# Attention and gated MLP on one core: a list scheduler in the source sets the order of all queues from the first MLP batch on

## The chip, the core and the metric

The kernel runs on one core of a Trainium2 chip. The metric is the device time in microseconds of one execution. The core has five engines with a queue of instructions each, which an engine works off in order: TensorE (PE in the profile; its weight loads are PEld), VectorE (DVE), ScalarE (ACT), GpSimd (POOL) and SyncE (SP), which here only issues DMAs. An engine waits at an instruction until the semaphores that it needs are there, and what stands behind it in the queue waits with it.

## The reference, cut to what matters

```python
scores = scale * np.matmul(q, k.transpose(0, 1, 3, 2))          # 8 batches, 8 heads, 576 tokens, 64 wide
cum = np.cumsum(np.log(np.clip(f, 0.0001, 1.0)), axis=-1)
decay = cum[:, :, :, None] - cum[:, :, None, :]
scores = np.where(causal, -1000000000.0, scores + decay)
attn = np.exp(scores - np.max(scores, axis=-1, keepdims=True))
attn = attn / (np.sum(attn, axis=-1, keepdims=True) + 1e-09)
x = np.matmul(attn, v)                                          # heads side by side: 576 x 512 a batch
h = np.maximum(x @ w_in, 0.0)                                   # 512 -> 1024
u, v = h[..., :512], h[..., 512:]
v_n = (v - mu) / np.sqrt(var + 1e-06)                           # mean and variance over the 512
v_s = np.einsum('ts,bsd->btd', w_spatial, v_n) + b_spatial[None, :, None]
return (u * v_s) @ w_out
```

## The kernel before, in words

Two heads form a pair; there are 32 pairs, four to a batch (`PPB`). The attention of pairs 0 to 3 and the scores of pair 4 run alone in `first` (about 74 us, ordered by hand). After that a loop at the end of the function draws from two generators, `attention(b)` and `moe(b)` (the gated MLP of one batch), so that the attention of batch b+1 is written in between the MLP of batch b. Within each queue the framework's scheduler then sets the order, from the order of the source and from its own estimate of durations.

A pair goes this way. SyncE loads `qk_t`, the decay rows `dk` and `dt`, and `vraw` (`prep`, `prep_v`). GpSimd masks `dk` and `dt` (`mask`, L280, L282, L286). TensorE makes the **first score piece** (three blocks of 128 queries with 384, 256 and 128 keys, L326, `sc<-qk_t`), then the **512 piece** (L326), then two **tail products** (queries 512 to 575 of both heads, `sc<-qk_t` with 288 columns, L233, since the helper `mm` records them). VectorE adds the decay and finds the row minimum (`lowest`, L306), ScalarE exponentiates and sums (L337; the tail L375), VectorE inverts the sums (L352, L353), and GpSimd multiplies the weights by them (`share`, L314). This multiplication I call a **share**; a pair has eight on `tt` and one on `tl`. They come after the 512 piece, since all four sums of a head are inverted together.

The weights must then be transposed. For pairs 0 to 7 TensorE does that (L414, L425) and ScalarE copies the result to `e` (L405). From pair 8 on (`moved`) VectorE transposes 32x32 blocks into `mid` (`move`, L456, L381) and SyncE puts the blocks in place with 16 DMAs from `mid` to `e` (`send`, L463); these need the product of the pair before to be done with `e`. The **product** with `vraw` (L480, from pair 8 on L488 and L493) writes two PSUM banks, which ScalarE (`xh`, L510) and VectorE (`xl`, L513) empty; `xh` and `xl` are the two fp32r parts of x.

The MLP of a batch multiplies in three terms (`xh winh`, `xh winl`, `xl winh`), all recorded as L233 with `ps`, `tp` or `sc` as target: first the v half token by token (`winh,xh` in the profile), followed by relu (L773), statistics (L774, L775), the root on GpSimd (L776, L777), normalization (`vx<-vx,mv`, L778) and the split into `vnh` (L780) and `vnl` (L782); then the u half (`xh,winh`); then the spatial product with `sph`, `spl`; then u times v_s (L823), its split into `gh` (L826) and `gl` (L827), and the product with `woh`, `wol`, copied to `o` and stored (L851, L853). In the first MLP batch the remaining weights are loaded and split too (`load_rest`, L126 to L144).

Of the kernel before, what the change touches and what calls it, by code (L numbers as in the profile page):

```python
# [15 lines left out]
PSUM = bass.MemoryType.PSUM  # L16
# [16 lines left out]

def f32(ap):
    return ap.bitcast(F32)


@with_exitstack
def attn_gmlp_kernel(ctx: ExitStack, tc: tile.TileContext, qk, v, f, w_in, w_sp, b_sp, w_out, out):
# [5 lines left out]
    nc = tc.nc  # L45
# [14 lines left out]
    ident = cst.tile([128, 128], F32, name="ident")  # L60
# [127 lines left out]
    own = {}  # L188
# [14 lines left out]
    def behind(i, j, sync=False):  # L203
        tc.add_manual_dep(i.ins, j.ins.name, mybir.DependencyInfo(
            mybir.DependencyClass.Sync if sync else mybir.DependencyClass.NoSync, mybir.DependencyReason.DATA),
            reason="order")

    freed, banks = {}, []

    def bank(n, piece=True):  # L210

# [5 lines left out]
    def in_one_piece(jobs, needs=()):  # L217

        was = None
        for job in jobs:  # L220
            if was is None:
                was = job()
                for j in [freed[n] for n in banks if n in freed] + list(needs):
                    behind(was, j, sync=True)
            else:
                with tc.high_priority():
                    i = job()
                behind(i, was)
                was = i
        banks.clear()  # L230

# [626 lines left out]
    def step(gen, done, t):  # L858
        try:
            return done + next(gen) / t, True  # L860
        except StopIteration:
            return round(done), False

    with tc.tile_pool(name="ws", bufs=2) as ws, tc.tile_pool(name="p0s", bufs=1, space=PSUM) as p0s, \
            tc.tile_pool(name="p0t", bufs=2, space=PSUM) as p0t:
        PS['s'], PS['t'] = p0s, p0t
        ws_.append(ws)
        first(ws)
        da, on = 1.0, False
    mo = ctx.enter_context(tc.tile_pool(name="mo", bufs=1, reuse_waits="tile"))  # L870
    for k, n in (("s", 1), ("t", 2)):
        PS[k] = ctx.enter_context(tc.tile_pool(name="ps_" + k, bufs=n, space=PSUM, reuse_waits="tile"))
    ps_m = ctx.enter_context(tc.tile_pool(name="ps_m", bufs=2, space=PSUM, reuse_waits="tile"))
    for b in range(B):
        gm = moe(b)
        dm, mon = 0.0, True
        while mon:
            while da < min(B, b + 1 + LEAD + dm):
                if not on:
                    gen, on = attention(int(round(da))), True  # L880
                da, on = step(gen, da, t_attn if b else t_first)
            dm, mon = step(gm, dm, t_moe)


# [41 lines left out]
```

## Time and profile before

| | |
|---|---|
| time, median of 3 runs | 758.35 us (758.02 to 760.0) |
| the profiled execution's own time | 758.39 us |
| its span, first to last instruction | 756.4 us |
| TensorE busy | 698.5 us (92% of the span), 4709 matmuls |
| VectorE, GpSimd, ScalarE busy | 481.2, 378.0, 369.6 us |
| mean granted TensorE clock | 0.984 |

The busy time of TensorE counts a matmul until its modelled end, so short waits between two of them don't show in it. The span is cut below into the part that `first` takes (to 74 us), the first MLP batch (to 160 us), the regular run of pairs and MLP batches (to 700 us) and the last MLP batch, in which no attention is left.

### The profile page before, as it was taken

What the parts mean: (1) busy time and instruction counts of PE and PEld (TensorE: products, weight loads), DVE (VectorE), ACT (ScalarE), POOL (GpSimd) and SP (SyncE); (2) the same over time, 40 slices, a digit from 0 to 9 for tenths busy, and PEclk for the clock granted to TensorE, in tenths of its full rate; (3) what the DMA queues carried; (4) which work ended last, traced back from release to release, by engine and by line L of the source; (5) the groups of instructions that cost most, each with busy time, mean ns of one, the idle gap of its engine ahead of it and who ended that gap; (6) DMA issues with size and microseconds to landing.
All of it is one profiled execution on the core that took longest, in us unless ns stands there. A gap on an engine that the chain in (4) does not pass through costs nothing.

```text
span 756.4 us, 14604 instructions
## 1 busy us (share of the span) xinstructions
PE 698.5 (92%) x4709; PEld 556.3 (74%) x4709; DVE 481.2 (64%) x1597; ACT 369.6 (49%) x1028; POOL 378.0 (50%) x703
## 2 busy tenths in 40 slices
PE   7878978799999998999998999999998898999997
PEld 3555757567788876877776877887787776788996
DVE  5888777954686648756776547756775556862421
ACT  5876686763544454533453344534563434641421
POOL 2887545582654426444644337354543446541411
PEclk9999999999999999999999999999999999999999
DMA  7855345245746865777576675776675675544001
GB/s 224 234 160 152 100 143 153 78 130 157 203 120 183 204 172 140 175 209 191 155 199 173 154 202 142 185 201 178 193 188 135 177 197 144 155 115 106 29 1 69
DMA packets 52749, 117.82 MB, mean 156 GB/s; under 512 B 10305, under 2 KB 14401, under 8 KB 52674
## 3 DMA queue, kind: packets, MB, share of 16 engines
q1 hardware_dynamic: 48082, 108.64, 53.8%
q10 hardware_dynamic: 4592, 8.26, 3.2%
q8 instruction: 37, 0.61, 0.4%
q14 instruction: 38, 0.31, 0.1%
HBM read 67.78 MB, written 9.75 MB: 102 GB/s over the span
## 4 chain that ended last, share of the span: by engine, by line
PE 41%; POOL 11%; DVE 9%; issue 8%; DMA 6%; ACT 5%; SPq 3%; POOLq 0%; ACTq 0%; DVEq 0%
PE ps L233 15%; PE tp L233 13%; POOL tt L314 5%; PE sc L326 5%; PE sc L233 4%; DMA dt<-rows_d 3%; PE sc L488 3%; ACT tt L337 3%; SPq L463 3%; DVE mid L456 2%; DMA dk<-rows_d 2%; DMA e<-mid 1%; DVE tt L306 1%; POOL vnl L782 1%; POOL gl L827 1%
## 5 line engine op out<-in xcount | busy, mean ns | idle before, releaser
L337 ACT ACTIVATE tt<-tt,nm 128x384 f32<-128x384 f32 (+2 forms) x240 | 132.7, 554 | 66.0 <-DVE nm L306 58.9
L314 POOL TENSOR_SCALAR tt<-tt,sm 128x128 f32<-128x128 f32 x208 | 108.0, 539 | 37.2 <-DVE sm L353 37.0
L456 DVE STREAM_TRANSPOSE mid<-tt 128x128 f32<-128x128 f32 x192 | 93.1, 500 | 40.3 <-POOL tt L314 34.6
L827 POOL TENSOR_TENSOR gl<-u,gh 128x256 fp32r<-128x256 f32 (+1 forms) x64 | 51.5, 805 | 107.3 <-ACT gh L826 106.7
L326 PE MATMUL sc<-qk_t 64*128 64x128 f32 (+3 forms) x512 | 90.1, 471 | 14.7 <-DVE xl L513 9.0
L306 DVE CUSTOM_DVE_ANT_1 tt<-sc,dk 128x256 f32<-128x256 f32 (+1 forms) x120 | 64.8, 550 | 23.1 <-PE sc L326 20.0
L326 PEld LDWEIGHTS sc<-qk_t 64*128 64x128 f32 x512 | 45.2, 190 | 39.1 <-DVE xl L513 11.3
L488 PE MATMUL sc<-e,vraw 128*64 128x256 f32 (+1 forms) x576 | 65.6, 348 | 4.6 <-DVE nm L306 1.7
L306 DVE CUSTOM_DVE_ANT_0 tt<-sc,dk 128x128 f32<-128x128 f32 (+1 forms) x120 | 48.8, 419 | 24.2 <-PE sc L326 22.6
L826 ACT CAST gh<-u 128x256 fp32r<-128x256 f32 (+1 forms) x64 | 27.0, 428 | 71.1 <-DVE u L823 34.6
L510 ACT CAST xh<-sc 128x256 fp32r<-128x256 f32 x64 | 25.1, 398 | 55.7 <-PE sc L488 31.9
L780 ACT CAST vnh<-vx 128x512 fp32r<-128x512 f32 (+1 forms) x40 | 24.7, 619 | 51.9 <-DVE vx L778 51.7
L782 POOL TENSOR_TENSOR vnl<-vx,vnh 128x512 fp32r<-128x512 f32 x32 | 41.3, 1298 | 15.0 <-ACT vnh L780 14.8
L776 POOL TENSOR_TENSOR mv<-mv,lnc 128x1 f32<-128x1 f32 (+1 forms) x40 | 8.4, 214 | 79.6 <-DVE mv L775 79.6
L280 POOL TENSOR_SCALAR_AFFINE_SELECT dk<-dk 128x256 f32<-128x256 f32 x60 | 25.4, 423 | 45.0 <-DMA dk<-rows_d 44.8
L233 PE MATMUL ps<-xh,winh 128*128 128x320 f32 (+1 forms) x136 | 42.9, 319 | 3.8 <-DVE vx L772 2.2
L774 DVE BATCH_NORM_STATS2 st<-vx 128x6 f32<-128x512 f32 (+1 forms) x40 | 27.1, 684 | 28.6 <-ACT vx L773 28.4
L337 ACT ACTIVATION_READ_ACCUMULATOR tt<-tt,nm 128x1 f32 x240 | 45.1, 188 | 0.0
L233 PE MATMUL sc<-qk_t 128*128 128x288 f32 x128 | 42.1, 425 | 1.9 <-DVE nm L306 1.9
L233 PE MATMUL ps<-sph,vnh 128*128 128x256 f32 (+1 forms) x144 | 43.8, 304 | 0.0
L233 PE MATMUL ps<-xh,winl 128*128 128x320 f32 (+1 forms) x136 | 41.3, 305 | 2.6 <-POOL winl L144 2.6
L488 PEld LDWEIGHTS sc<-e,vraw 128*64 128x64 f32 x576 | 32.4, 137 | 15.0 <-issue 4.9
(230 smaller groups left out, 2067.9 us busy)
## 6 DMA issues: line engine op xcount, KB each, us to landing
e<-mid SPq DMA_DIRECT2D x384, 100.0 KB, 2.2
qk_t<-in_dram SPq DMA_DIRECT2D x32, 608.0 KB, 6.6
dk<-rows_d SPq DMA_DIRECT2D x58, 320.0 KB, 4.4
vraw<-in_dram SPq DMA_DIRECT2D x32, 320.0 KB, 4.3
dt<-rows_d SPq DMA_DIRECT2D x58, 144.0 KB, 6.5
out_dram<-o ACTq DMA_DIRECT2D x28, 256.0 KB, 2.5
w<-in_dram SPq DMA_DIRECT2D x16, 256.0 KB, 3.0
w<-in_dram SPq DMA_DIRECT2D x4, 512.0 KB, 6.7
```

The source lines that it names most:

```text
L233: T.matmul(o, l, r, start=st, stop=sp)
L280: G.affine_select(out=two, in_=two, compare_op=ALU.is_ge, fill=-8.0 * BIG, base=0, pattern=[[0, 2], [-1, 128]], channel_multiplier=1)
L306: return V.tensor_tensor_reduce(out=out, in0=ps, in1=dec, scale=-0.125, scalar=3.0e38, op0=ALU.add, op1=ALU.min, accum_out=acc_)
L314: G.tensor_scalar(out=t, in0=t, scalar1=r, scalar2=1.0, op0=ALU.mult, op1=ALU.mult)
L326: return lambda: T.matmul(ps[:, c:c + n], qk_t[p, n - 128:n], qk_t[p, 640:640 + n], start=True, stop=True)
L337: last["exp", P, h, i] = A.activation(t, t, AF.Exp, bias=nm, scale=-1.0, accum_out=sm)
L456: V.transpose(out=part(middle(P)[:, 0, at:], [[32, n], [RUN, 4], [1, 32]]), in_=part(t, [[128, n], [32, 4], [1, 32]]))
L488: return lambda: T.matmul(out, vt[:, c, h, :], src, start=c == 0, stop=c == end)
L774: V.bn_stats(out=st[m, :], in_=x[m, :])
L782: G.tensor_tensor(out=tlo, in0=x, in1=f32(th[:]), op=ALU.subtract)
L826: A.copy(gh[j][:, 0:nt], g)
L827: G.tensor_tensor(out=gl[j][:, 0:nt], in0=g, in1=f32(gh[j][:, 0:nt]), op=ALU.subtract)
```

## The change

The new function `in_queues` runs at the end of the kernel function over all instructions written so far. It makes a step of every instruction (a score piece or a product is one step), finds what each step depends on from the memory it touches, gives it a duration by a table of linear costs (`cost`) and a delay until another engine sees its end (`SEEN`), and plans: at each turn it takes the engine that can start a ready step first, and of that engine's ready steps the one with the lowest rank. In the first plan the rank is the place in the source; then, three times, it is the latest start that still meets the end (`latest`), worked out backwards along the dependences and along TensorE's queue. A step that needs a new buffer waits until one of its kind is free (`PLACES`). Steps from before the first MLP batch count as done at time 0, with all engines free. The last plan's order is then laid down for each queue by dependences that order without a semaphore. No instruction's work is changed.

```diff
+PLACES = dict(GH=3, U=9, vnh=5, vnl=4, vx=2, st=2, mv=2, o=2, qk=2, xh=6, xl=6, nm=6, sm=6, tp=2, ps=2)
+SEEN = {"PE": 150, "DVE": 24, "Activation": 23, "Pool": 66, "SP": 17}
...
+def cost(i, e, ins, outs):
+
+    n = max([elements(b.ap) for b, _ in outs + (ins if i.opcode == "BNStats" else [])] or [1])
+    psum = any("PSUM" in str(b.tensor.space) for b, _ in ins)
+    op = str(getattr(i, "op", "")).split(".")[-1]
+    if i.opcode == "DMACopy":
+        name = outs[0][0].tensor.name.split("_")[0]
+        return {"e": 640, "out": 400}.get(name, 540), {"e": 2450, "qk": 5900, "raw": 5900, "dk": 4700, "dt": 5500,
+                                                     "vraw": 4000}.get(name, 3250)
...
+def in_queues(nc, tc, start, pieces, needs):
+
+    steps, of, own = [], {}, {i: p[0] for p in pieces for i in p[1:]}
+    W, R, users, tag_of, kinds = {}, {}, {}, {}, {}
+    for j, i in enumerate(nc.cur_bb.bb.instructions):
...
+    def lag(n, q):
+        return n.busy if n.e == q.e and not n.dma else n.done + SEEN[q.e]
+
+    def run(rank):
+
+        ready, free, mode = {e: [] for e in SEEN}, dict.fromkeys(SEEN, 0.0), None
+        when, at, left = [0.0] * len(steps), [0.0] * len(steps), [len(n.pred) for n in steps]
+        order, todo = {e: [] for e in SEEN}, {t: list(reversed(l)) for t, l in kinds.items()}
...
+        for _ in range(sum(not n.early for n in steps)):
+            best = None
+            for e, l in ready.items():
+                c = [(t, n) for n in l for t in (can(n),) if t is not None]
+                if c:
+                    t = max(free[e], min(t for t, _ in c))
+                    if best is None or t < best[0]:
+                        best = t, e, c
+            s, e, c = best
+            n = min((n for t, n in c if t <= s), key=lambda n: (rank[n.k], n.k))
+            ready[e].remove(n)
+            free[e] = s + n.busy
+            if e == "PE":
+                free[e] += 92 * (n.mode != mode)
+                mode = n.mode
+            at[n.k] = s
+            order[e].append(n)
+            take(n, s + n.done)
+            leave(n, s)
+        return at, order
+
+    def latest(at, order):
+
+        end = max(at[n.k] + n.done for n in steps if not n.early)
+        due, after = [end] * len(steps), {a.k: b for a, b in zip(order["PE"], order["PE"][1:])}
+        for n in sorted(steps, key=lambda n: -at[n.k]):
+            due[n.k] = min([end - n.done] + [due[q.k] - lag(n, q) for q in n.succ] +
+                           [due[q.k] - n.busy for q in (after.get(n.k),) if q])
+        return due
+
+    at, order = run([n.k for n in steps])
+    for _ in range(3):
+        at, order = run(latest(at, order))
+    for l in order.values():
+        l = [i for n in l for i in n.ins]
+        for a, b in zip(l, l[1:]):
+            tc.add_manual_dep(b, a.name, mybir.DependencyInfo(
+                mybir.DependencyClass.NoSync, mybir.DependencyReason.DATA), reason="order")
...
-    freed, banks = {}, []
+    freed, banks, pieces, needed = {}, [], [], []
...
+    early = len(nc.cur_bb.bb.instructions)
     mo = ctx.enter_context(tc.tile_pool(name="mo", bufs=1, reuse_waits="tile"))
...
                 da, on = step(gen, da, t_attn if b else t_first)
             dm, mon = step(gm, dm, t_moe)
+    in_queues(nc, tc, early, pieces, needed)
```

Where the change moves instructions is seen in the lists of the queues. On GpSimd, at the shares of pair 13, before (`tt_84` and `tt_85` are the weights of the two heads, `dk` the decay of pair 14):

```order
L280 AFFINE_SELECT dk<-dk 128x2x128
L314 TENSOR_SCALAR tt_84<-tt_84,sm 128x128
L782 TENSOR_TENSOR vnl<-vx,vnh 128x512
L314 TENSOR_SCALAR tt_84<-tt_84,sm 128x256
L314 TENSOR_SCALAR tt_84<-tt_84,sm 128x384
L314 TENSOR_SCALAR tt_84<-tt_84,sm 128x512
L314 TENSOR_SCALAR tt_85<-tt_85,sm 128x128
L314 TENSOR_SCALAR tt_85<-tt_85,sm 128x256
L314 TENSOR_SCALAR tt_85<-tt_85,sm 128x384
L314 TENSOR_SCALAR tt_85<-tt_85,sm 128x512
L282 AFFINE_SELECT dk<-dk 128x256
```

The same place in the changed kernel:

```order
L526 TENSOR_SCALAR tt_84<-tt_84,sm 128x384
L526 TENSOR_SCALAR tt_84<-tt_84,sm 128x256
L526 TENSOR_SCALAR tt_85<-tt_85,sm 128x384
L526 TENSOR_SCALAR tt_85<-tt_85,sm 128x256
L526 TENSOR_SCALAR tt_84<-tt_84,sm 128x128
L526 TENSOR_SCALAR tt_85<-tt_85,sm 128x128
L526 TENSOR_SCALAR tt_84<-tt_84,sm 128x512
L526 TENSOR_SCALAR tt_85<-tt_85,sm 128x512
L492 AFFINE_SELECT dk<-dk 128x2x128 x2
L494 AFFINE_SELECT dk<-dk 128x256 x2
L526 TENSOR_SCALAR tl<-tl,sm 128x576
```

The first mask of the next pair stood ahead of all shares and now stands behind the eight on `tt`. Over the 24 moved pairs a mask had four or more of the nine shares behind it in 20; now in 4, and in most of the others the last one or two.

On VectorE, at the moves of the same pair and the `xl` of pair 12, before:

```order
L456 STREAM_TRANSPOSE mid_2223<-tt_84 128x2x4x32
L456 STREAM_TRANSPOSE mid_2223<-tt_84 128x3x4x32
L456 STREAM_TRANSPOSE mid_2223<-tt_84 128x4x4x32
L456 STREAM_TRANSPOSE mid_2223<-tt_85 128x4x32
L456 STREAM_TRANSPOSE mid_2223<-tt_85 128x2x4x32
L456 STREAM_TRANSPOSE mid_2223<-tt_85 128x3x4x32
L513 TENSOR_TENSOR xl<-sc,xh 128x256
L456 STREAM_TRANSPOSE mid_2223<-tt_85 128x4x4x32
L513 TENSOR_TENSOR xl<-sc,xh 128x320
```

The same place in the changed kernel:

```order
L668 STREAM_TRANSPOSE mid_2223<-tt_85 128x4x32
L586 TENSOR_TENSOR nm<-nm 128x1
L986 BN_STATS st<-vx 128x6
L668 STREAM_TRANSPOSE mid_2223<-tt_84 128x4x4x32
L588 TENSOR_TENSOR sm<-sm,eps 128x1
L589 RECIPROCAL sm<-sm 128x1
L668 STREAM_TRANSPOSE mid_2223<-tt_85 128x4x4x32
L986 BN_STATS st<-vx 128x6
L725 TENSOR_TENSOR xl<-sc,xh 128x320
L725 TENSOR_TENSOR xl<-sc,xh 128x256
L668 STREAM_TRANSPOSE mid_2223<-tl 128x4x4x32
L593 STREAM_TRANSPOSE mid_2223<-tl 128x2x32
```

`xl` stands behind most moves in both; its two halves now come one behind the other, and the two moves of the tail close the pair.

On TensorE, from the first tail product of pair 14 to its 512 piece, before:

```order
L233 MATMUL sc<-qk_t 128x288
L233 MATMUL tp<-xh,winh 128x256
L233 MATMUL tp<-xh,winl 128x256
L233 MATMUL tp<-xl,winh 128x256
L233 MATMUL tp<-xh,winh 128x256
L233 MATMUL ps<-xh,winh 128x320
L233 MATMUL ps<-xh,winl 128x320
L233 MATMUL ps<-xl,winh 128x320
L233 MATMUL ps<-xh,winh 128x320
L326 MATMUL sc<-qk_t 128x512 x2
```

The same stretch in the changed kernel, from the 512 piece to the first tail product:

```order
L538 MATMUL sc<-qk_t 128x512 x2
L445 MATMUL ps<-xh,winl 128x320
L445 MATMUL ps<-xl,winh 128x320
L445 MATMUL ps<-xh,winh 128x320
L445 MATMUL ps<-xh,winl 128x320
L445 MATMUL ps<-xl,winh 128x320
L445 MATMUL sc<-qk_t 128x288
```

The 512 piece now comes first. In 9 of the 24 moved pairs the first tail product stood ahead of it; now in none.

## Rows read from the trace of the kernel before

**Rows 1.** The first line of the page.
```profile
span 756.4 us, 14604 instructions
```

**Rows 2.** Busy us of each engine (instructions) by stretch, clock, DMA share, GB/s.
```profile
74.00:160.00 86.00, 72.64 (x465) 55.05 (x462) 66.34 (x201) 58.27 (x167) 52.48 (x89) 0.96 0.42 124
160.00:700.00 540.00, 517.09 (x3583) 418.87 (x3582) 342.98 (x1172) 243.65 (x686) 259.02 (x494) 0.99 0.64 169
700.00:756.40 56.40, 51.38 (x312) 46.62 (x310) 15.91 (x37) 15.30 (x31) 15.30 (x22) 1.00 0.09 33
500.00:550.00 50.00, 50.00 (x349) 40.14 (x346) 31.35 (x112) 21.04 (x59) 26.44 (x54) 1.00 0.68 189
```

**Rows 3.** Waits of PE from 160 to 700 us: total us, times, longest.
```profile
PE sc L326 <- DVE xl L513: 8.0, 6, 2.7
PE tp L233 <- POOL gl L827: 2.8, 1, 2.8
PE ps L233 <- POOL gl L827: 2.2, 1, 2.2
PE ps L233 <- DVE vx L772: 2.0, 2, 1.0
```

**Rows 4.** Timeline of all engines, 281 to 297 us: start, duration, instruction, idle before.
```profile
283.66 0.41 POOL L280 TENSOR_SCALAR_AFFINE_SELECT dk<-dk 128x256 f32<-128x256 f32 x1 [3.24 <-DMA dk<-rows_d]
...
285.66 3.74 POOL L314 TENSOR_SCALAR tt<-tt,sm 128x256 f32<-128x256 f32 x7
...
286.61 2.73 DVE L456 STREAM_TRANSPOSE mid<-tt 128x256 f32<-128x256 f32 x6
...
290.19 0.45 DVE L513 TENSOR_TENSOR xl<-sc,xh 128x320 fp32r<-128x320 f32 x1
...
290.70 1.57 PE L326 MATMUL sc<-qk_t 64*128 64x384 f32 x12 [1.34 <-DVE xl L513]
```

**Rows 5.** Busy time by stretch around one long wait.
```profile
588.00:590.00 2.00, 0.00 (x0) 0.00 (x0) 1.86 (x6) 1.32 (x4) 2.00 (x5) 1.00 1.05 236
...
592.00:594.00 2.00, 2.00 (x9) 2.00 (x9) 1.25 (x4) 0.59 (x1) 0.92 (x2) 0.51 0.58 219
```

**Rows 6.** Two matmuls of PE, one behind the other.
```profile
285.40 0.39 PE L233 MATMUL tp<-winh,xl 128*128 128x512 f32 x1
285.63 0.40 PE L233 MATMUL ps<-winh,xh 128*128 128x512 f32 x1
```

**Rows 7.** Tail products of pair 14 on PE.
```profile
301.44 0.65 PE L233 MATMUL sc<-qk_t 128*128 128x288 f32 x2
```

**Rows 8.** SyncE’s queue from 300 to 345 us.
```profile
312.95 11.30 SPq L463 DMA_DIRECT2D e<-mid  x16
```

**Rows 9.** Pair 14’s product on PE, first and last row.
```profile
326.28 0.65 PE L488 MATMUL sc<-e,vraw 128*64 128x256 f32 x4 [1.32 <-DVE sm L376]
...
328.82 0.40 PE L493 MATMUL sc<-e,vraw 128*64 128x64 f32 x7
```

**Rows 10.** Second tail product of pair 31 on PE.
```profile
672.36 0.65 PE L233 MATMUL sc<-qk_t 128*128 128x288 f32 x2
```

**Rows 11.** SyncE’s queue from 670 to 690 us.
```profile
678.27 10.79 SPq L463 DMA_DIRECT2D e<-mid  x16
```

**Rows 12.** DMA issues on the page: count, KB, median us to landing.
```profile
e<-mid SPq DMA_DIRECT2D x384, 100.0 KB, 2.2
...
dk<-rows_d SPq DMA_DIRECT2D x58, 320.0 KB, 4.4
```

**Rows 13.** Timeline of all engines, 281 to 297 us, two normalizations.
```profile
292.57 0.51 DVE L778 TENSOR_SCALAR vx<-vx,mv 128x512 f32<-128x512 f32 x1
...
293.80 1.59 DVE L778 TENSOR_SCALAR vx<-vx,mv 128x512 f32<-128x512 f32 x1 [0.71 <-POOL mv L777]
293.81 1.30 POOL L782 TENSOR_TENSOR vnl<-vx,vnh 128x512 fp32r<-128x512 f32 x1
```

**Rows 14.** Timeline of POOL at the start of the first MLP batch.
```profile
74.55 1.36 POOL L314 TENSOR_SCALAR tt<-tt,sb 128x512 f32<-128x512 f32 x2
```

More of the change, by code (lines that the diff above doesn't have):

```diff
@@ L35, in f32, with __init__, elements @@
     return ap.bitcast(F32)
+PLACES = dict(GH=3, U=9, vnh=5, vnl=4, vx=2, st=2, mv=2, o=2, qk=2, xh=6, xl=6, nm=6, sm=6, tp=2, ps=2)
+SEEN = {"PE": 150, "DVE": 24, "Activation": 23, "Pool": 66, "SP": 17}
+class Step:
+    def __init__(self, k, e):
+        self.k, self.e, self.ins, self.pred, self.succ, self.tiles = k, e, [], set(), [], []
+        self.busy = self.done = 0.0
+        self.mode = self.dma = None
+def elements(ap):
+    n = 1
+    for _, k in ap[1:]:
+        n *= k
+    return n
@@ new lines, in touched @@
+def touched(b):
+    pitch = b.ap[0][0] or 1
+    at = [b.offset % pitch]
+    for s, k in b.ap[1:]:
+        at = [x + s * j for x in at for j in range(k)]
+    mask = 0
+    for x in at:
+        mask |= 1 << (x >> 2)
+    return b.offset // pitch, b.offset // pitch + b.ap[0][1], mask
+def cost(i, e, ins, outs):
[7 more added lines that the diff above has]
+    if e == "PE":
+        rows, cols = i.tile_size
+        slow = str(ins[0][1]) == "dt.float32"
+        if any(b.tensor.name.startswith("ident") for b, _ in ins):
+            t = 107
+        elif rows > 64 and cols > 64:
+            t = max(218, n * 1.667 + 8) if slow else max(111, n * 0.425 + 14)
+        else:
+            t = max(43, n * 0.888) if slow else max(55, n * 0.208 + 1)
+        return t, n * (0.92 if slow else 0.417) + 180
+    if e == "Activation":
+        t = (280 if len(outs) > 1 else 50 if psum else 185 if i.opcode == "Activation" else 100) + 0.83 * n
+        return t, t + 105
+    if e == "DVE":
+        t = 105 if n < 8 else (95 if i.opcode == "StreamTranspose" else 70) + (
+            0.8 if i.opcode == "TensorScalarPtr" else 1.06) * n
+        return t, t + 95
+    if i.opcode == "TensorTensor":
+        t = 520 if op == "pow" else 140 if n < 8 else 60 + 2.47 * n
+    else:
+        t = (240 if i.opcode == "TensorScalarPtr" else 140) + 0.84 * n
+    return t, t + 38
@@ L222, in in_one_piece @@
                 was = job()
+                pieces.append([was.ins.name])
                 for j in [freed[n] for n in banks if n in freed] + list(needs):
                     behind(was, j, sync=True)
+                    needed.append((was.ins.name, j.ins.name))
             else:
@@ L228, in in_one_piece @@
                 behind(i, was)
+                pieces[-1].append(i.ins.name)
                 was = i
```

86 lines of the change are left out of this document (added).

## The prediction

> **What bounds the kernel now.** I read the page first (span 756.4 us against 758.39 us for that execution, so 2.0 us lie outside the span) [rows 1], then the busy time by stretch [rows 2], then the waits of TensorE, and last the timeline at single waits. The reader should see in [rows 2] that TensorE is the engine that counts and that it is not always fed. From 160 to 700 us it is busy 517.09 of 540 us while VectorE is busy 342.98 and GpSimd 259.02, so these two have room on average. From 500 to 550 us it is busy 50.00 of 50 us at the full clock: the same work without waits exists in this very trace. From 74 to 160 us, where the remaining weights are split beside attention and MLP, it is busy only 72.64 of 86 us.
>
> What an order can give back is bounded by two things. Idle time: 86.00 - 72.64 = 13.4 us and 540.00 - 517.09 = 22.9 us. Clock: after an idle stretch (588 to 590 us, no matmul at all) TensorE was busy all of 592 to 594 us at a granted clock of 0.51, which is the lower level, 1.2 GHz [rows 5]. A wait of two microseconds is thus paid again in part. Over the two stretches the clock is 0.96 and 0.99 [rows 2], so at most 0.04 x 86 = 3.4 and 0.01 x 540 = 5.4 us. Together 45.1 us. The 5.0 idle us after 700 are the end of the program, where both orders do the same MLP, and the first 74 us are not touched by the planner.
>
> The waits are of a kind that an order makes. From 160 to 700 us TensorE's longest total is for `xl` before a first score piece, 8.0 us in 6 waits; then two single waits for `gl` of 2.8 and 2.2 us, the last subtraction ahead of the output product; 2.0 us for `vx`; 1.7 us for the row minimum that frees a tail product's bank [rows 3]. The idle time is 22.9 us, so some of it is spread over rows too small to list here, or shows only at weight loads.
>
> How one of them arises is in [rows 4]. At 283.66 us GpSimd starts the first mask of pair 14 after 3.24 us of waiting for the DMA of `dk`. The shares of pair 13 stand behind it, and seven of them run at 285.66 us. VectorE's six moves follow at 286.61 us; the second `xl` of pair 12 stands behind these moves and runs at 290.19 us; and the score piece, which needs the bank that `xl` reads, starts at 290.70 us after 1.34 us of idle TensorE. A DMA that TensorE does not need yet has held it up through two queues.
>
> **What the change does, part by part.**
>
> *Work.* No instruction is added or removed; the matmuls of the two queues add up to the same. 0 us.
>
> *GpSimd.* The masks no longer stand ahead of the shares in most pairs (20 of 24 before had four or more shares behind a mask, now 4 of 24). A wait like the 3.24 us [rows 4] then holds at most one or two shares and the tail. This is the main gain, since the shares feed the moves, the moves hold `xl`, and `xl` holds the score pieces.
>
> *TensorE's distances.* I add up TensorE's own work between two places in each order: 0.23 us for a 512-column matmul (start to start) and less in proportion [rows 6], 1.5 us for a first score piece [rows 4], about 0.5 us for a tail product (two records, overlapped by their ends) [rows 7], and 2.8 us for a pair's product (326.28 to 328.82 us and its last rows) [rows 9]. From the end of a product to the first score piece two pairs on, there were 3.9 to 7.0 us in 23 of the 24 moved pairs; now 4.7 to 6.8 in 19, with 1.6, 2.6, 3.4 and 3.4 as exceptions and one of 10.8. The chain there (copy, subtraction) is short if VectorE's queue is on time: 0.4 to 0.5 us for an `xl` [rows 4]. In 9 of 24 pairs the first tail product stood ahead of the 512 piece; now it follows by 0.7 to 2.2 us always, which gives the row minimum time. I expect the waits for `xl` and for the row minimum to go.
>
> *What gets tighter.* A pair's product needs all 16 sends of that pair, and these need the last move. In the old order 20.7 to 26.5 us of TensorE's work lie between the end of the second tail product and the product; in the new one 19.9 to 20.9 in 20 pairs and 16.9 to 18.1 in four. What the chain takes: the tail product of pair 14 ends at 301.44 + 0.65 = 302.1 us, the sends begin at 312.95, so 10.9 us later, take 11.30 us, and the product starts 2.0 us after them [rows 7 to 9]. That is 24.2 us, and this product was late: TensorE had been idle for 1.32 us. At pair 31, with no MLP statistics in the way, the sends begin 678.27 - 673.0 = 5.3 us after the tail product [rows 10, 11]. With 10.79 us of sends [rows 11] and the same 2.0 us this is 18.1 us, and a landing of 2.2 us at the median [rows 12] agrees with the last step. So the new order works if the sends begin within 20 - 13 = 7 us of the tail product. The trace has both ends, 5.3 and 10.9 us. Since the long one has the 3 us of mask waiting in its kind of queue and the new order removes that in most pairs, I take it nearer the short end, about 7 us, but with a spread: I charge 0.4 us of waiting in each of 24 pairs, 10 us. Bounds: nothing (5.3 us everywhere) and 24 x 3.9 = 94 us (10.9 us everywhere, which the masks' new place speaks against).
>
> *SyncE.* The sends are now 16 in one piece, ahead of the next `dk`, as before in most pairs. `dk` lands 4.4 us after issue [rows 12]. It is hidden while the masks come late; where one stands ahead of the last two shares, its lateness goes into the sends, and that is in the 0.4 us.
>
> *The seam.* The planner takes all engines as free at the first MLP matmul. The last shares of pair 4 end at 74.55 + 1.36 = 75.9 us [rows 14], while the new TensorE queue puts seven transposes of these weights behind the first three matmuls, 0.7 us after 74.1. I charge 1 us (bounds 0 and 2, the latter if the copies to `e` are late as well).
>
> *Weights split (74 to 160 us).* Here the waits have many causes (copies, splits, shares), and a planner that knows durations should fill a good part by pulling transposes and scores ahead, as it does from the first matmuls on. I take 60% of 13.4 + 3.4 = 16.8: 10 us. Bounds 3 and 15.
>
> *Sum.* 10 us up to 160; 22.9 + 5.4 - 10 = 18.3 us from there to 700; less 1 us at the seam: 27.3 us. 758.39 - 27.3 = 731.1 us, by the profiled time, which is the median (758.35) but for 0.04. **Predicted 731 us.** Its own range, from half to three quarters of the 45.1 us: 725 to 736.
>
> **A rule against it.** `vx` took 0.51 us at 292.57 and 1.59 us at 293.80, where it started with GpSimd's `vnl` (293.81, 1.30 us) [rows 13]; VectorE had to wait inside the instruction. The planner's table has one price for it. If each of the 32 whole normalizations ran beside `vnl`, VectorE would lose 32 x 1.08 = 35 us; it has 197 idle us from 160 to 700, so on TensorE's path only the last one or so of each batch counts, 8 x 1.08 = 9 us: 740 us. The Trainium skill (GPSIMD Engine Reference, section Key points) says that GpSimd shares its SBUF interfaces with VectorE and that they contend with VectorE instructions in a two-port mode or with two SBUF inputs. By that rule a tighter packing of the two engines lengthens both; the two rows agree with it for this one operation.
>
> **The rivals.**
> - *The waits move to the products* (sends late by 1 us rather than 0.4): 24 us are given back in place of 10, 745 us. For it: the sends of pair 14 already ended right ahead of their product [rows 8, 9], and three of the new distances lie below the 18.1 us. Against: a late product also delays everything behind it, which gives the next pair's sends more time.
> - *VectorE's normalizations stretch* (above): 740 us. For it [rows 13]; against, that they already do so before.
> - *Nearly all comes back*: 716 us, with 3 us of waits left. For it, the 50 us without a wait [rows 2]; against, that queues in a fixed order lose whenever one step is late and never win when it is early.
> - *No change* (758 us, within 0.3%): the order would have to lose as much as it wins, 1.1 us in each of 24 pairs on top of the 0.4.
> - *Slower*: the place is the product again. If the sends begin 9 us after the tail product, each product waits 2 us, and the clock falls behind such a wait [rows 5] for about 1 us more: 24 x 3 = 72 us lost against 37 us won elsewhere (10 + 28.3 - 1), 793 us at worst; with half of the pairs, 757. It decides from about 1.5 us of waiting a pair.
>
> **How the numbers follow.** Forecast 0.52, products 0.17, VectorE 0.09, nearly all 0.11, no change 0.04, slower 0.07. The first four are faster by over 0.3% (2.3 us, about what three runs can tell from no change): 0.89. The range leaves out the no-change and slower cases and the ends of the outer two: 714 (the floor is 713.3) to 748, a little beyond the products' case.
>
> **What would show it.** In the profile after: TensorE's busy time in 160 to 700 us closer to the length of the stretch, the wait for `xl` before score pieces gone or below 2 us, the waits of GpSimd for `dk` no longer followed by waits of VectorE for shares, first sends 6 to 8 us behind the tail product, and small waits at the products instead. The prediction is wrong if products wait over 1 us in most pairs, if the stretch to 160 us keeps its idle 13 us, or if waits shorter than the profile's idle rows show make the gain larger than 45 us.

## The result, and the profile after

The changed kernel takes 747.38 us (median of 4 runs, 746.35 to 747.91) where the kernel before takes 758.24 us beside it (median of 4, 758.02 to 760.0): a ratio of 0.985, with a 95% interval of 0.983 to 0.987. It is faster, by 11 us and not by the 27 us of the forecast, and the time lies at the upper end of the range. A second measurement, beside other runs of the kernel before, gave a ratio of 0.990 (0.986 to 0.993).

The first rows are the busy time by stretch of the profiled execution after the change (span 746.0 us), to be held against [rows 2]: length, then busy us of TensorE, weight loads, VectorE, ScalarE and GpSimd, each with its instructions, then TensorE's clock, DMA share and GB/s.

```profile
74.00:160.00 86.00, 71.28 (x447) 53.89 (x443) 70.92 (x193) 56.64 (x158) 52.19 (x81) 0.96 0.41 124
160.00:700.00 540.00, 525.70 (x3649) 425.62 (x3646) 341.02 (x1189) 252.98 (x699) 267.36 (x510) 0.99 0.65 171
```

From 160 to 700 us TensorE's idle time fell from 22.9 to 14.3 us. From 74 to 160 us it didn't fall at all: 14.7 us in place of 13.4. The starts of two pieces that have the same place in TensorE's work in both orders say the same: pair 11's first score piece starts at 227.1 us (before 225.8), pair 31's at 652.6 us (before 662.5). All of the gain lies between these two.

The waits of TensorE from 160 to 700 us, against [rows 3]: what waited for what, us in total, times, the longest.

```profile
PE tp L445 <- POOL gl L1039: 6.4, 3, 2.5
PE sc L538 <- DVE mv L987: 5.0, 5, 1.5
PE ps L445 <- POOL gl L1039: 1.8, 2, 1.4
PE sc L700 <- DVE mid L668: 0.6, 1, 0.6
```

The waits for `xl` are gone from the list, and the products (L700) wait 0.6 us in the whole stretch. But the waits for `gl` have grown from 5.0 to 8.2 us (6.4 and 1.8), and there is a new one: the 512 piece waits in each of five MLP batches, 5.0 us in sum, for a statistics step on VectorE. The largest wait for `gl`, on the timeline of GpSimd, SyncE and TensorE (start, duration, instruction, and in brackets the idle time before it with what ended it):

```profile
574.07 1.00 SPq L464 DMA_DIRECT2D dk<-rows_d  x2
...
578.71 0.41 POOL L492 TENSOR_SCALAR_AFFINE_SELECT dk<-dk 128x256 f32<-128x256 f32 x1 [0.79 <-DMA dk<-rows_d]
581.06 0.41 POOL L492 TENSOR_SCALAR_AFFINE_SELECT dk<-dk 128x256 f32<-128x256 f32 x1 [1.95 <-DMA dk<-rows_d]
581.42 0.77 POOL L494 TENSOR_SCALAR_AFFINE_SELECT dk<-dk 128x256 f32<-128x256 f32 x2
582.17 0.74 POOL L526 TENSOR_SCALAR tl<-tl,sm 128x576 f32<-128x576 f32 x1
582.89 0.69 POOL L526 TENSOR_SCALAR tt<-tt,sm 128x512 f32<-128x512 f32 x1
583.54 0.72 POOL L1039 TENSOR_TENSOR gl<-u,gh 128x256 fp32r<-128x256 f32 x1
...
584.32 0.50 PE L445 MATMUL tp<-woh,gl 128*128 128x512 f32 x1 [2.50 <-POOL gl L1039]
...
586.44 0.47 PE L445 MATMUL tp<-sph,vnh 128*128 128x320 f32 x1
586.71 0.47 PE L445 MATMUL tp<-spl,vnh 128*128 128x320 f32 x1
```

This is the pattern of [rows 4] once more, with other work behind it. GpSimd stands at a mask until the second `dk` lands, at about 581 us, 6.3 us after its issue in the trace (the plan's table says 4.7 for each `dk`; the first took 4.6). Behind the masks stand the tail share, the last share and `gl`, and TensorE waits 2.50 us for `gl`. Then it starts 320-column matmuls 0.27 us apart; in a kernel below, at the same place without the wait, 0.15 us apart. The granted clock behind the wait is 0.50, the lower level of 1.2 GHz:

```profile
585.00:588.00 3.00, 3.00 (x12) 2.80 (x11) 0.00 (x0) 1.03 (x2) 0.11 (x1) 0.50 0.75 192
```

The wait before the 512 piece is of the same make. At 374.65 us GpSimd starts a mask of `dt` after 2.30 us of waiting for its DMA. The two small steps on `mv` stand behind it, VectorE waits 2.85 us for them before its normalization, and the next statistics and the row minimum come after that; the 512 piece starts at 383.93 us after 1.51 us of idle TensorE.

```profile
374.65 0.23 POOL L498 TENSOR_SCALAR_AFFINE_SELECT dt<-dt 64x64 f32<-64x64 f32 x1 [2.30 <-DMA dt<-rows_d]
375.71 0.55 DVE L990 TENSOR_SCALAR vx<-vx,mv 128x512 f32<-128x512 f32 x1 [2.85 <-POOL mv L989]
```

### The profile page after: what moved, and what is told of

The parts are those of the page before. It is cut to its first block, busy times and chain, and to the rows that moved or that the text cites. A ratio compares the mean times of both kernels' runs of the same rounds, so it can differ in the third digit from the quotient of the medians.

```text
span 746.0 us, 14624 instructions
## 1 busy us (share of the span) xinstructions
PE 695.9 (93%) x4709; PEld 553.4 (74%) x4709; DVE 479.8 (64%) x1597; ACT 373.2 (50%) x1028; POOL 381.6 (51%) x703
## 4 chain that ended last, share of the span: by engine, by line
PE 62%; DVE 10%; POOL 7%; issue 4%; DMA 2%; ACT 1%; POOLq 0%; DVEq 0%; SPq 0%; ACTq 0%
PE ps L445 23%; PE tp L445 19%; PE sc L538 7%; PE sc L700 5%; PE sc L445 5%; POOL tt L526 3%; DVE tt L518 2%; PE sc L692 1%; PE sc L705 1%; DVE mid L668 1%; DMA dt<-rows_d 1%; DVE st L986 1%; POOL vnl L994 1%; POOL mv L989 1%; DVE vx L990 1%
## 5 line engine op out<-in xcount | busy, mean ns | idle before, releaser
L526 POOL TENSOR_SCALAR tt<-tt,sm 128x384 f32<-128x384 f32 (+3 forms) x208 | 110.4, 550 | 43.9 <-DVE sm L565 28.3
L538 PE MATMUL sc<-qk_t 64*128 64x128 f32 (+3 forms) x512 | 87.5, 460 | 9.9 <-DVE mv L987 5.0
L668 DVE STREAM_TRANSPOSE mid<-tt 128x384 f32<-128x384 f32 (+3 forms) x192 | 86.7, 486 | 9.7 <-POOL tt L526 8.7
L518 DVE CUSTOM_DVE_ANT_1 tt<-sc,dk 128x256 f32<-128x256 f32 (+1 forms) x120 | 62.2, 553 | 17.3 <-PE sc L538 17.0
L518 DVE CUSTOM_DVE_ANT_0 tt<-sc,dk 128x384 f32<-128x384 f32 (+1 forms) x120 | 46.8, 417 | 35.1 <-PE sc L538 33.5
L700 PE MATMUL sc<-e,vraw 128*64 128x256 f32 (+1 forms) x576 | 65.6, 348 | 0.7 <-DVE mid L668 0.6
L994 POOL TENSOR_TENSOR vnl<-vx,vnh 128x512 fp32r<-128x512 f32 x32 | 41.5, 1303 | 23.2 <-ACT vnh L992 22.9
L587 ACT ACTIVATE tl<-tl,nm 128x576 f32<-128x576 f32 x27 | 21.0, 777 | 51.4 <-DVE nm L586 51.4
L445 PE MATMUL ps<-spl,vnh 128*128 128x256 f32 (+1 forms) x144 | 42.5, 295 | 0.0
L445 PE MATMUL ps<-sph,vnl 128*128 128x256 f32 (+1 forms) x144 | 42.5, 295 | 0.0
```

What stands on the lines that cost most here:

```text
L445: T.matmul(o, l, r, start=st, stop=sp)
L518: return V.tensor_tensor_reduce(out=out, in0=ps, in1=dec, scale=-0.125, scalar=3.0e38, op0=ALU.add, op1=ALU.min, accum_out=acc_)
L526: G.tensor_scalar(out=t, in0=t, scalar1=r, scalar2=1.0, op0=ALU.mult, op1=ALU.mult)
L538: return lambda: T.matmul(ps[:, c:c + n], qk_t[p, n - 128:n], qk_t[p, 640:640 + n], start=True, stop=True)
L668: V.transpose(out=part(middle(P)[:, 0, at:], [[32, n], [RUN, 4], [1, 32]]), in_=part(t, [[128, n], [32, 4], [1, 32]]))
L700: return lambda: T.matmul(out, vt[:, c, h, :], src, start=c == 0, stop=c == end)
```

## The experiments

The idle times in the table are the length of the stretch less TensorE's busy time in each profile; the ratio is to the kernel before, run beside it on the same chip. The kernel before took 753.8 to 758.2 us in the five sets of runs, so the ratios are compared, not the times. The last column is the time from the first score piece of pair 4 to that of pair 11 in each profile. TensorE has the same matmuls between these two in all rows but the two with a star, where some more stand ahead of pair 11, about 3 us in the first and 8 us in the second (an estimate from 0.12 us between matmuls of 256 columns and 0.23 us between those of 512). Unlike idle time in a fixed window, this time also holds what a lower clock costs.

| Kernel | us | ratio (95%) | idle 74-160 | idle 160-700 | pair 4 to 11 |
|---|---|---|---|---|---|
| before | 758.24 | 1 | 13.4 | 22.9 | 164.8 |
| planned (the change) | 747.38 | 0.985 (0.983-0.987) | 14.7 | 14.3 | 166.2 |
| planned, second measurement | 747.18 | 0.990 (0.986-0.993) | 15.8 | 14.7 | 165.3 |
| prices of `dk` and `dt` raised | 731.48 | 0.971 (0.968-0.974) | 15.7 | 0.8 | 168.6 |
| price of `dk` alone | 730.42 | 0.969 (0.965-0.973) | 15.9 | 1.8 | 168.6 |
| price of `dt` alone | 740.41 | 0.982 (0.979-0.986) | 15.1 | 9.2 | 167.0 |
| raised, GpSimd's queue alone laid down | 730.66 | 0.969 (0.966-0.972) | 9.8 | 3.8 | 169.1* |
| raised, all queues but GpSimd's | 819.58 | 1.087 (1.084-1.091) | 16.9 | 57.6 | 179.8 |
| before, masks behind the last share from pair 9 | 731.99 | 0.973 (0.968-0.977) | 13.6 | 2.8 | 164.8 |
| the same from the first pairs on | 732.28 | 0.970 (0.966-0.974) | 12.7 | 2.7 | 165.8 |
| split priced double | 749.77 | 0.996 (0.993-0.999) | 17.9 | 14.7 | 170.3 |
| raised, split priced 1.3 times | 729.31 | 0.968 (0.964-0.971) | 16.2 | 0.7 | 168.0 |
| before, without VectorE's split | 742.89 | 0.986 (0.982-0.989) | 4.7 | 24.4 | 160.3* |
| planned, without VectorE's split | 740.08 | 0.982 (0.979-0.985) | 9.5 | 13.5 | 160.6 |
| raised, without VectorE's split | 717.70 | 0.952 (0.948-0.956) | 5.4 | 0.7 | 155.4 |
| raised, the maximum on GpSimd | 736.84 | 0.978 (0.974-0.981) | 17.3 | 2.2 | 171.8 |
| raised, without GpSimd's split | 726.54 | 0.963 (0.959-0.967) | 10.4 | 0.8 | 164.2 |

**Is the rest of the later stretch lost at the masks?** The table of landing times is all that is changed:

```
-"dk": 4700, "dt": 5500,
+"dk": 7500, "dt": 9000,
```

> The planned kernel with two prices raised in the table: the landing of `dk` 4700 to 7500, of `dt` 5500 to 9000. Theory 1 (what the later stretch lacks is lost where GpSimd's masks wait for a landing that the plan has too early, ahead of `gl` and of the two small steps on `mv`): TensorE's waits for `gl` at the output products and before the 512 piece, 14.9 us of idle in ten places by the timeline, shrink to below 4 us in all, the half clock behind them goes too, and the time falls by 8 to 14 us, to 733 to 740 us. Rival (a fixed order always meets some late step, whatever the prices): the waits turn up at other rows, the sum of idle time stays, and the time is 744 to 750 us. Up to 160 us both expect no change beyond 2 us.

Measured: 2.9% below the kernel before. Theory 1 holds. The stretch and the same place in the program as above:

```profile
160.00:700.00 540.00, 539.19 (x3793) 441.27 (x3790) 346.71 (x1201) 259.46 (x714) 271.48 (x515) 1.00 0.64 170
```

```profile
566.40 0.75 POOL L526 TENSOR_SCALAR tl<-tl,sm 128x576 f32<-128x576 f32 x1 [1.15 <-DVE sm L589]
567.45 0.74 POOL L1039 TENSOR_TENSOR gl<-u,gh 128x256 fp32r<-128x256 f32 x1 [0.30 <-ACT gh L1038]
568.14 0.41 POOL L492 TENSOR_SCALAR_AFFINE_SELECT dk<-dk 128x256 f32<-128x256 f32 x1
...
570.12 0.31 PE L445 MATMUL tp<-sph,vnh 128*128 128x320 f32 x1
570.27 0.31 PE L445 MATMUL tp<-spl,vnh 128*128 128x320 f32 x1
```

The tail share and `gl` now stand ahead of the masks, these find their `dk` landed, and TensorE is idle for 0.8 of 540 us at the full clock. No other wait took the place of those removed, as the rival had it.

Then each price alone.

> The planned kernel with the price of `dk` alone raised (4700 to 7500), that of `dt` left at 5500. Theory 1 (each wait has its own transfer: `gl` behind the masks of `dk`, the 512 piece behind the mask of `dt`): the waits for `gl` at the output products go (9.0 of 14.9 us), those of the 512 piece stay at 5 of 1.0 to 1.7 us, and the time is 1.9 to 2.5% below the kernel before. Rival (the place of the masks of `dk` decides over both): as with both prices raised, 2.7 to 3.1% below.

> The planned kernel with the price of `dt` alone raised (5500 to 9000), that of `dk` left at 4700. Theory 1, as mended by the run with `dk` alone (the masks of `dk` decide; those of `dt` follow them in the queue): the waits of the 512 piece for `mv` go, those for `gl` behind the masks of `dk` stay at 4 to 9 us, and the time is 1.6 to 2.4% below the kernel before. Rival (either price moves the masks far enough back): 2.7 to 3.1% below.

Measured: `dk` alone gives 3.1%, all of it, and of the waits of the 512 piece for `mv` one of 0.3 us is left; so "each wait has its own transfer" was wrong. `dt` alone gives 1.8% and leaves 5.7 us of waits for `gl`, as the mended theory expects, though 2.8 us for `mv` stay too, which it expected to go. The masks of `dt` follow those of `dk`, so the price of `dk` decides.

**Whose order brings the gain?** The same plan, laid down for a part of the queues (the first new line in one kernel, the second in the other):

```
-    for l in order.values():
+    for l in [order["Pool"]]:
+    for l in [order[e] for e in order if e != "Pool"]:
```

> The plan with the raised prices is made for all queues, but laid down for GpSimd's alone; the others take the order that they get without a plan. Theory of the prediction (the new place of the masks on GpSimd is the main gain, since shares feed moves, moves hold `xl`, and `xl` holds the score pieces): 11 us or more of the 22 us come, 1.5 to 2.5% below the kernel before, and the wait for `xl` before score pieces is below 3 us. Rival (the gain needs TensorE's new distances too): less than 5 us, 0 to 0.7% below the kernel before.

> The same plan laid down for all queues but GpSimd's. Theory of the prediction: with masks back ahead of shares over half of the 22 us is lost, 0.3 to 1.4% below the kernel before. Rival (TensorE's order carries the gain and draws GpSimd's queue after it): 2.2 to 3% below the kernel before.

Measured: GpSimd's queue alone gives 3.1%, all of the gain and more than the theory of the prediction expected (the framework's scheduler sets the other queues around it). All the other queues without it make the kernel 8.7% slower than before, worse than either expectation. In its trace GpSimd again has the first mask of `dk` ahead of four or more shares, in 11 pairs; but the kernel before has that in 20 and isn't as slow. The likely reason is that the others now stand in a fixed order that counts on GpSimd's planned one, so that each late share or `gl` holds up more; no run shows that by itself. GpSimd's waits from 160 to 700 us in that kernel:

```profile
POOL dk L492 <- DMA dk<-rows_d: 45.6, 22, 6.2
POOL dt L498 <- DMA dt<-rows_d: 34.9, 25, 3.0
```

and what TensorE then waits for:

```profile
PE tp L445 <- POOL gl L1039: 12.5, 4, 4.4
PE sc L538 <- DVE xl L725: 11.8, 6, 4.7
PE ps L445 <- POOL gl L1039: 8.9, 2, 4.7
```

**Are the masks enough?** No planner, one order by hand in the kernel before (`shared[P]` is the last share of a pair, its tail share):

```
 def mask(P, part=None):
     ...
+    if moved(P - 1):
+        for i in masks:
+            behind(i, shared[P - 1])
```

> The kernel before, without any planner, with one order added by hand: from pair 9 on every mask of a pair stands behind the last share of the pair before it on GpSimd. Theory 3 (the place of the masks is all of the gain from 160 us on; the list scheduler is only a way to find it): the waits for `xl` and for `gl` go, from 160 to 700 us TensorE is idle 4 us or less instead of 22.9, and the time is 2.2 to 3.2% below the kernel before. Rival (the other shifts on GpSimd that the plan makes, of `gl`, of the normalization and of the shares among themselves, are needed too): idle time of 8 to 16 us there, 0.8 to 1.9% below.

> The kernel before with the masks behind the last share of the pair before from the first pairs on, not only from pair 9 on; no planner. If the masks have no part in the stretch up to 160 us: within 0.4% of the same order from pair 9 on, 2.3 to 3.2% below the kernel before, TensorE idle there 12 to 15 us. If they have: idle 9 us or less there, 3.3 to 4% below.

Measured: 2.7% from pair 9 on, 3.0% from the first pairs on, idle time from 160 to 700 us 2.8 and 2.7 us, and no wait above 0.9 us in all from there (the first two rows of TensorE's waits, masks from pair 9 on):

```profile
PE sc L332 <- DVE xl L519: 0.9, 2, 0.7
PE sc L332 <- DVE nm L312: 0.7, 2, 0.3
```

Theory 3 holds: three lines (and the lists that name the instructions for them) do what the list scheduler does with the raised prices. The intervals overlap, so which is faster can't be told. The masks have no measurable part in the stretch up to 160 us: pair 11's first score piece comes 164.8 and 165.8 us after pair 4's, as before.

**Why did the stretch up to 160 us give nothing?** In the planned kernel VectorE is busy 70.92 of these 86 us. Its weight-split operations are longer beside GpSimd than alone. Eight rows of VectorE, GpSimd and TensorE in the planned kernel:

```profile
106.87 0.29 DVE L344 TENSOR_SCALAR wa<-wa 128x256 uint32<-128x256 uint32 x1
106.89 0.87 POOL L353 TENSOR_TENSOR winl<-w,winh 128x256 fp32r<-128x256 f32 x1 [0.84 <-ACT winh L352]
107.20 0.84 DVE L345 SCALAR_TENSOR_TENSOR w<-w,wa 128x256 uint32<-128x256 uint32 x1
107.72 1.45 POOL L994 TENSOR_TENSOR vnl<-vx,vnh 128x512 fp32r<-128x512 f32 x1
...
110.53 1.33 POOL L994 TENSOR_TENSOR vnl<-vx,vnh 128x512 fp32r<-128x512 f32 x1
110.76 1.26 DVE L344 TENSOR_SCALAR wa<-wa 128x256 uint32<-128x256 uint32 x1
112.11 0.42 DVE L345 SCALAR_TENSOR_TENSOR w<-w,wa 128x256 uint32<-128x256 uint32 x1
...
114.80 0.75 PE L445 MATMUL sc<-qk_t 128*128 128x288 f32 x2 [2.49 <-DVE nm L518]
```

L344 takes 0.29 us, and 1.26 us where it meets `vnl`; L345 takes 0.42 us, and 0.84 us where it meets GpSimd's L353, the last operation of another split. Behind them in VectorE's queue stand the row minima, and TensorE waits 2.49 us for one. First other prices for the five operations, 2.0 times with the first prices of the rows and 1.3 times with the raised ones. The table has 275 ns for each; with the raised prices they took 478 ns on average (38.2 us for 80), so that the two factors lie on both sides of the measured 1.74:

```
+        if n == 256 and i.opcode == "TensorScalarPtr":
+            t *= 2.0
```

> The planned kernel with one price changed: VectorE's operations of the weight split (256 elements, a scalar operand) cost double. Theory 2 (up to 160 us VectorE itself is too full, its split operations being stretched beside GpSimd, so an order can't win there): pair 11's first score piece starts at 227 us as in the planned kernel, within 2 us, and the time is 745 to 750 us. Rival (the order of that stretch is bad because the plan doesn't know the length of those operations): with the right price it is filled better, the piece starts 5 to 10 us earlier, and the time falls to 737 to 742 us.

> The plan with the raised prices, and VectorE's operations of the weight split priced at 1.3 times. Theory 2 (VectorE is full there, so a better price doesn't help): within 0.4% of the raised prices alone, 2.5 to 3.3% below the kernel before. Rival (a right price, unlike the double one, lets the plan fill the stretch): 3.5% or more below.

Measured: the double price gains nothing. It is 0.4% below the kernel before where the planned one is 1.0 to 1.5% below it, though its interval touches that of the second measurement, and pair 11 comes 170.3 us after pair 4, 4 to 5 us later than with the plan (in the profile its piece starts at 234.8 us). Theory 2 expected no change, the rival a gain. With 1.3 times nothing changes, as theory 2 has it. A price nearer the measured one doesn't help. Then the operations left out, in three orders:

```
-        V.tensor_scalar(out=af, in0=af, scalar1=2.0 ** -15, scalar2=None, op0=ALU.max)
-        V.tensor_scalar(out=a, in0=a, scalar1=3, scalar2=0x3FFFFFF8, op0=ALU.logical_shift_left, op1=ALU.bitwise_and)
-        V.scalar_tensor_tensor(out=w, in0=hi, scalar=0xC0000000, in1=a, op0=ALU.bitwise_and, op1=ALU.bitwise_or)
-        V.tensor_scalar(out=a, in0=w, scalar1=0xFF800000, scalar2=None, op0=ALU.bitwise_and)
-        V.scalar_tensor_tensor(out=af, in0=lo, scalar=2.0 ** -52, in1=af, op0=ALU.mult, op1=ALU.mult)
+        A.activation(wf, hi.bitcast(F32), AF.Abs)
```

> The kernel before, with VectorE's five operations of each of the 16 weight splits after the first 74 us left out (one more absolute value on ScalarE stands in for them), so that these weights are not the reference's. It takes 80 operations off VectorE, 40 us by their durations in the planned kernel. Theory 2 (VectorE is what fills the stretch up to 160 us): the stretch gets shorter by 5 to 10 us even in the old order, and the time is 748 to 754 us. Rival (the waits up to 160 us come from copies, landings and the order): 755 to 759 us.

> The planned kernel with the same operations left out, so that these weights are not the reference's. Theory 2: the plan now gets there what was forecast for it, TensorE's idle time from 74 us to pair 11 falls by some 10 us, and the time is 733 to 739 us, 12 to 18 us below the old order with the same operations left out. Rival (something else than VectorE holds the stretch up): 742 to 748 us, and the distance between the two orders stays at 11 us.

> The planned kernel with the raised prices of `dk` and `dt` and, as in the two kernels before it, without VectorE's five operations of each of the 16 later weight splits, so that these weights are not the reference's. With the raised prices TensorE is busy 499.19 of 500 us from 160 us on, so nothing later can hide or eat what the first stretch gives. Theory 2 (VectorE's stretched split operations make the stretch up to 160 us late): idle time there falls from 15.7 us to 9 us or less, and the time is 6 to 9 us below that of the raised prices, 3.6 to 4.1% below the kernel before. Rival (the planned order itself leaves TensorE without work there, whatever VectorE does): within 3 us of the raised prices, 2.6 to 3.3% below the kernel before.

Measured: in the old order 1.4%, a little more than theory 2 expected, and an idle time of 4.7 us up to 160 us; with the raised prices 4.8%, so 1.9% or 14 us more than the plan with these operations, twice what theory 2 expected. In the planned kernel with its first prices the idle time fell by 5.2 us only, and the two orders came within 0.4% of each other, which neither theory expected: the plan there loses 5.0 us up to 160 us at ScalarE's copies to `e`. Why it does so with these prices and not with the raised ones wasn't tried. The stretch with the raised prices, with and without the five operations:

```profile
74.00:160.00 86.00, 70.32 (x432) 54.19 (x432) 67.94 (x189) 55.47 (x156) 52.50 (x85) 0.92 0.39 123
```

```profile
74.00:160.00 86.00, 80.61 (x517) 63.28 (x517) 36.66 (x121) 65.22 (x189) 55.03 (x95) 0.96 0.43 134
```

So it is the split's operations on VectorE. Leaving them out also makes each split five steps shorter, though, and these three kernels alone can't tell VectorE's time from that. The waits of TensorE in the plan with the raised prices speak for VectorE's time (74 to 162 us, the five largest):

```profile
PE ps L445 <- ACT u L1013: 4.4, 2, 4.2
PE sc L538 <- DVE nm L518: 2.8, 1, 2.8
PE sc L538 <- DVE xl L725: 2.3, 1, 2.3
PE sc L692 <- DVE nm L518: 2.1, 2, 1.9
PE ps L445 <- DVE vx L984: 2.0, 1, 2.0
```
```profile
128.43 0.24 ACT L735 CAST xh<-xl 128x64 fp32r<-128x64 f32 x1 [2.21 <-DVE xl L725]
```

Four of the five end at VectorE, and before the long one for `u` ScalarE had itself stood 2.21 us waiting for VectorE's `xl`; none ends at a split weight. (In the old order one of 2.6 us does, for `winl`.) Is it the amount of VectorE's work, or the stretching? Two edits of the later splits: one of the five operations moved to GpSimd, and, in another kernel, GpSimd's two operations left out:

```
-        V.tensor_scalar(out=af, in0=af, scalar1=2.0 ** -15, scalar2=None, op0=ALU.max)
+        G.tensor_scalar(out=af, in0=af, scalar1=2.0 ** -15, scalar2=1.0, op0=ALU.max, op1=ALU.mult)
```
```
-        G.tensor_tensor(out=wf, in0=wf, in1=af, op=ALU.add)
-        G.tensor_tensor(out=dl, in0=wf, in1=f32(dh), op=ALU.subtract)
+        A.copy(dl, af)
```

> The plan with the raised prices, and one of VectorE's five operations of each later weight split, the maximum, done by GpSimd. Theory 2 (VectorE's load makes the stretch up to 160 us late; leaving all five out gave 14 us): a fifth of it, 2 to 4 us, 3.1 to 3.5% below the kernel before, with VectorE busy 5 to 8 us less from 74 to 160 us. Rival (what stretches VectorE's operations is GpSimd's work beside them, and more of that takes as much as it gives): no gain, 2.5 to 3.0% below.

> The plan with the raised prices, with GpSimd's two operations of each of the 16 later weight splits left out (ScalarE's copies stand in for one of them), so that these weights are not the reference's. It takes 32 operations of 0.73 us off GpSimd and none off VectorE. Theory 2a (VectorE is stretched by GpSimd's work beside it): VectorE's 80 split operations, 38.2 us in sum with the raised prices, take 31 us or less, idle time of TensorE up to 160 us falls from 15.7 us by 5 us or more, and the time is 3.6 to 4.4% below the kernel before. Theory 2b (it is the amount of VectorE's work): their sum stays above 34 us, or it falls and the idle time stays within 3 us; 2.5 to 3.3% below.

> The planned kernel as it is, on the chip of the runs beside it. All theories expect what it measured before, 1.3 to 1.7% below the kernel before, and so 8 to 11 us above the same plan with the raised prices.

Measured: with the maximum on GpSimd the kernel is 2.2% below the one before, less than either side expected and 0.6% worse than without that edit, though VectorE is busy 9 us less in the stretch. Moving work from VectorE to GpSimd doesn't make it faster. Without GpSimd's part it is 3.7% below, 0.8% better, and idle time falls by 5.3 us. VectorE's groups in this stretch (count, busy us, mean ns), first with the raised prices alone, then without GpSimd's part:

```profile
L345 DVE SCALAR_TENSOR_TENSOR w<-w,wa 128x256 uint32<-128x256 uint32 x16 | 9.4, 586 | 0.9
L344 DVE TENSOR_SCALAR wa<-wa 128x256 uint32<-128x256 uint32 x16 | 7.3, 453 | 0.5
L342 DVE TENSOR_SCALAR wa<-wa 128x256 f32<-128x256 f32 x16 | 6.6, 412 | 2.2 <-ACT wa L340 2.1
```

```profile
L345 DVE SCALAR_TENSOR_TENSOR w<-w,wa 128x256 uint32<-128x256 uint32 x16 | 8.0, 503 | 1.0 <-ACT winh L353 0.4
L344 DVE TENSOR_SCALAR wa<-wa 128x256 uint32<-128x256 uint32 x16 | 5.9, 368 | 0.5
L342 DVE TENSOR_SCALAR wa<-wa 128x256 f32<-128x256 f32 x16 | 4.8, 303 | 3.5 <-ACT wa L340 3.5
```

All 80 operations took 38.2 us and now take 32.5, between the two bounds. By time and idle time theory 2a fits. But the run also takes two steps out of each split's chain and gives GpSimd 22 us back (busy 52.50 before, 30.61 now), so how much of the 0.8% is the shorter operations and how much the shorter chain stays open. The planned kernel as it is came out at 1.0% below the one before, less than the 1.3 to 1.7% expected, and so 1.9% or 14 us above the raised prices, where 8 to 11 us were expected.

## Why the prediction was right and wrong

*The mechanism was right.* The masks on GpSimd hold shares, moves, `xl` and score pieces; "the main gain" was put there. GpSimd's queue alone, or three lines in the kernel before, bring all of the gain that any order brought. The waits for `xl` went as forecast. VectorE's waits for shares, from 160 to 700 us, fell from 56.5 to 17.7 us, but the chain from a late `dk` through a share to VectorE was not gone: behind the masks at 581 us VectorE still waited 2.55 us for the tail share. In the new trace four or more shares stand behind the first mask of the next pair's `dk` in one pair, where four were counted in advance.

*The step that failed* is "I take 60% of 13.4 + 3.4 = 16.8: 10 us" for the stretch up to 160 us. It measured nothing: idle time 14.7 for 13.4 us, clock 0.96 as before, pair 11 1.3 us later. That the stretch keeps its idle 13 us was one of the prediction's own signs of being wrong. The idle rows there were read as an order's fault. But VectorE was busy 66.34 of 86 us there [rows 2] and its split operations stretch beside GpSimd. Taking these away freed 8.7 us even in the old order (13.4 to 4.7), and 10.3 us in the plan with raised prices. No order or price tried there gave that: GpSimd's queue alone shows 9.8 us of idle time, but at a clock of 0.88, and pair 11 comes no earlier than in the kernel before (169.1 us after pair 4, with about 3 us more work ahead of it). The rival "VectorE's normalizations stretch" names a lengthening that the rows up to 160 us show as well, for other operations; from 160 us on VectorE had room enough for it (idle 0.8 us in the plan with raised prices, with the same operations), and up to 160 us, where it hadn't, the prediction didn't look for it. How much of the loss is the lengthening and how much the amount of VectorE's work stays open. The Trainium skill (SBUF — State Buffer, section Who interferes with whom) says that VectorE and GpSimd share a port pair that one of them holds for a whole instruction while the other is blocked, and that `tensor_scalar` can need it. The rows agree: L344 at 110.76 us ended 0.16 us after the `vnl` that had started 0.23 us before it.

*The term of 18.3 us* from 160 to 700 us was right in kind and came out at about 11 us (from pair 11 to pair 31: 9.9 + 1.3). What was charged against it, 10 us of small waits at the products, was wrong in place and in size: the products waited 0.6 us. In their stead about 13 us were waited for `gl` and before the 512 piece, and the half clock came behind some of these waits. The prediction saw that a mask could still stand ahead of the last two shares, as it does in 15 pairs of the trace, and put "its lateness into the sends"; it didn't follow GpSimd's queue on to `gl` and to the steps on `mv`, which stand behind the masks as well. With the masks' price mended, all 22.9 us of the idle rows but 0.8 came back, and the time from pair 11's first score piece to pair 31's fell from 436.7 to 407.0 us, by 29.7. So the 28.3 us from idle time and clock were a sound measure of what an order can give back in this stretch, and "nearly all comes back" was the right case for it, once the plan knew how long a landing takes.

*The sends.* The first sends began 4.8 to 9.5 us behind the tail product in the planned kernel, 17 of 24 within the 6 to 8 us that were named, and the products waited 0.6 us in all: the 7 us taken from the bounds 5.3 and 10.9 held, and the 0.4 us a pair charged on top did not come. The rival that the products take over the waits, and the slower case that rests on it, fall.

*The seam.* It was charged as 1 us, and from 74 to 80 us TensorE is idle for 0.6 us, waiting for a copy to `e`, where it had no idle time before. The rise from 74 to 100 us, from 1.5 to 5.0 us, is for the larger part two waits for row minima behind it, 1.56 and 2.43 us, which belong to the step that failed: VectorE is busy 9.26 us from 90 to 100 us.

## What to carry to other kernels

Where an in-order engine does work that waits for a DMA, look at what stands behind it in that queue, all of it and not only the first victim; a dependency of three lines that puts such work last did as much here as a scheduler for all queues with its best prices. A plan is as good as its longest waits are priced: a landing priced near the median of all put everything behind a mask at the mercy of the second of two transfers, and a landing priced too long cost little here (2 to 3 us from pair 4 to pair 11, against 18 us gained behind it). Before idle time is booked as an order's to give back, check that the engine it waits for has room in that very stretch, with the durations that its operations have there.

## What the runs showed of the hardware

Two transfers of `dk`, issued one behind the other in 1.00 us, landed 4.6 and 6.3 us after their issue in the case shown. VectorE's `tensor_scalar` from SBUF to SBUF on 128x256 took 0.29 us and up to 1.26 us beside GpSimd, its `scalar_tensor_tensor` 0.42 and 0.84 us; taking 22 us of GpSimd's work away made 80 of them 5.7 us shorter, and giving GpSimd one of the five didn't pay although VectorE had 9 us less to do. After a wait of 2.50 us TensorE started 320-column matmuls 0.27 us apart at a granted clock of 0.50, and 0.15 us apart at the same place without the wait.
